# Sums of squares of batches 2 to 4: accumulating DMA transfers in place of VectorE additions

## The chip, the cores and the metric

The kernel runs on one core of one Trainium2 chip, in one launch. The metric is the device time of that launch in microseconds (us), as the median of repeated runs; lower is better.

## What is computed

Channel attention over 4 batches of 6080 tokens with 256 channels, followed by a feed-forward layer with a squared ReLU. Queries and keys are normalised over the tokens, so each batch needs the sum of squares of every channel of q and of k over all 6080 tokens.

```python
qn = q / (norm(q, axis=1) + 1e-06)            # per channel, over the tokens
kn = k / (norm(k, axis=1) + 1e-06)
s = kn.transpose(0, 2, 1) @ qn / tau          # 256 x 256 per batch
a = softmax(s)                                # along the last axis
x = (v @ a).reshape(4 * 6080, 256)
h = maximum(x @ w_in, 0.0)                    # 2048 wide
out = (h * h) @ w_out
```

## The kernel before

The attention matrix of a batch is folded into w_in first (`fold`, `fold7`), so that the large work is two layers of matrix products over v. Each layer uses Strassen's seven products, and every float32 operand is split into a high and a low part of type float32r, so that one product is three matmuls. Tokens are worked in chunks of up to 1024 (6 per batch), and a chunk in 8 steps over the hidden width. Such a step is called a quad; there are 192 (4 batches, 6 chunks, 8 steps), and quad n counts the time of the plan.

A quad issues on TensorE the products of its first layer (L600) interleaved with the second layer of the quad before (L722, or L757 and L799 for the steps that are paired). ScalarE and VectorE empty the banks (L642, L651, L664, L669), square the ReLU (L615, L616, L629) and split the results (L619, L620, L630, L631).

Beside it runs side work for the next batch: `at(u, fn, ...)` gives a step a due time in quads, `run_side` issues the due steps between the products, and `pinned` ties each to ScalarE and VectorE instructions issued some 0.9 quads before. The framework then sets the final order on each engine from priorities, dependencies, buffers that come free and its own estimates of durations; each engine and each DMA queue works its list in order.

The side work for batch b (1 to 3 in the code, counted from 0; the batches 2 to 4 of the title) begins with the scores. Keys and queries come in as tiles `kqt` of four token rows per partition (L202, SyncE's queue). For every pair of rows, `score_split` splits them (L225, L226), `score_burst` issues 12 matmuls (L240), and `score_norm` squares them on ScalarE into a 128x1024 tile `sq` (L219) and adds that on VectorE to the running sum `acc` (L220). The first pair is squared straight into `acc` (L216). That makes 23 additions a batch and 92 in all; batch 0 runs them at the start of the kernel, before the quads.

The tag `sq` has two buffers. They also serve `combine_parts` (L505 to L519), `norms_wide` (L318), `attnT` and `fold7`. When all pairs are in, `squares_split` adds the two halves of `acc` (L303), and norms, exponentials and folds follow. The folded weights are split into tiles `wt` and stored to HBM as `wsc` by GpSimd's queue (POOL; L521); SyncE's queue loads them again one quad at a time (L527). The same POOL queue stores `tsc` (L459) and the outputs (L743).

The pacing of the side work, which sets when a square is due:

```python
first, last = (NJ + 2 if b == 1 else 0), 30
for i in range(NT // 2):                       # NT = 48
    u, k = u0 + first + i * (last - first) // (NT // 2), 2 * i
    ...
    at(u - 0.8, score_norm, b, k)
```

Of the kernel before, what the change touches and what calls it, by code (L numbers as in the profile page):

```python
# [13 lines left out]
ALU = mybir.AluOpType  # L14
# [6 lines left out]
def tile_channel_attention_relu2_ffn(ctx, tc, kq, vT, tau, w_in, w_out, outT):  # L21
# [15 lines left out]
    nc = tc.nc  # L37
# [155 lines left out]
    accs = {}  # L193
# [16 lines left out]
    def score_norm(b, kt):  # L210

        g, t = divmod(kt, G)
        x = kqt[b, g][:, t:t + 2]
        if kt == 0:
            accs[b] = small.tile([P, 2, C2], F32, name="acc")
            nc.scalar.activation(out=accs[b], in_=x, func=AF.Square)  # L216
        else:
            sq = work.tile([P, 2, C2], F32, name="sq", tag="sq")
            nc.scalar.activation(out=sq, in_=x, func=AF.Square)  # L219
            nc.vector.tensor_add(out=accs[b], in0=accs[b], in1=sq)  # L220

    def score_split(b, kt):
        x = kqt[b, kt // G][:, kt % G, :]
# [624 lines left out]
    for kt in range(NT):  # L848
        g = kt // G
        if kt % G == 0 and g < NGK - 1:  # L850
            for t in range(0, G, 2):
                score_norm(0, kt + t)
        if kt == NT - LAST:
            for t in range(0, G, 2):
                score_norm(0, NT - G + t)
            with tc.high_priority():
                summed = sums_of_squares(0)
            decoded = decode_w_in(0)
            with tc.high_priority(), tc.issue_after(decoded):
                scaled = norms(0)  # L860
            with tc.issue_after(scaled):
                fold_split(0, 0)
        with ExitStack() as order:
            if kt >= NT - LAST:
                order.enter_context(tc.issue_after(summed))
            score_mm(0, kt, s0, kt == 0, kt == NT - 1)
        if kt == 3 * G - 1:
            load_tau()
        if kt % G == G - 1:
            load_next()  # L870
# [63 lines left out]
    for b in range(1, B):  # L934
        u0 = (b - 1) * QB
        first, last = (NJ + 2 if b == 1 else 0), 30
        for i in range(NT // 2):
            u, k = u0 + first + i * (last - first) // (NT // 2), 2 * i
            if k % G == 0:
                at(u - 3.4, score_load, b, k // G)  # L940
            at(u - 0.8, score_norm, b, k)
            if b > 1 or k > LATE[-1]:
                at(u - 1.0, score_split, b, k)
                at(u - 0.5, score_split, b, k + 1)
                at(u + MID, score_burst, b, [k, k + 1])
        end = u0 + last
        at(end - 0.6, squares_split, b)
        at(end + MID, norms_wide, b)
        at(end + 1.6, lambda b=b: exps(b, s_acc[b]))
        at(end + 2 + MID, attnT, b)  # L950
        for g in range(0, NG, 2):
            u = end + 3 + 3.5 * g
            if b == 1:
                at(u - 3.5, load_wins2, g)
            for i in range(NP):
                at(u + i - (0.7 if b == 1 else 2.5), right7, b, g, i)
                at(u + i + MID, fold7, b, g, i)
            for i in range(2):
                at(u + NP + 2 * i, combine, b, g + i)
                at(u + NP + 2 * i + 1, combine, b, g + i)  # L960
# [88 lines left out]
```

## Time and profile before

| | us |
|---|---|
| median of 3 runs | 2147.49 |
| lowest and highest of them | 2146.72, 2148.78 |
| the profiled execution's own time | 2145.74 |
| span of its trace | 2143.9 |

| engine | busy us | share of the span |
|---|---|---|
| TensorE matmul (PE) | 2137.1 | 100% |
| TensorE weight load (PEld) | 1764.3 | 82% |
| VectorE (DVE) | 1822.0 | 85% |
| ScalarE (ACT) | 1451.9 | 68% |
| GpSimd (POOL) | 89.9 | 4% |

Times are microseconds from the span's start unless marked ns. "Landing" of a DMA is the time from its issue until its last byte is reported. Matmuls are pipelined and their ends are modelled, so a full TensorE row says that no gap was seen and not that the engine is at its peak. A name such as `acc<-acc,sq` gives the tile written and the tiles read. An idle time is put down to whatever came last before the instruction started.

### The profile page before, as it was taken

What the parts mean: (1) busy time and instruction counts of PE and PEld (TensorE: products, weight loads), DVE (VectorE), ACT (ScalarE), POOL (GpSimd) and SP (SyncE); (2) the same over time, 40 slices, a digit from 0 to 9 for tenths busy, and PEclk for the clock granted to TensorE, in tenths of its full rate; (3) what the DMA queues carried; (4) which work ended last, traced back from release to release, by engine and by line L of the source; (5) the groups of instructions that cost most, each with busy time, mean ns of one, the idle gap of its engine ahead of it and who ended that gap; (6) DMA issues with size and microseconds to landing.
All of it is one profiled execution on the core that took longest, in us unless ns stands there. A gap on an engine that the chain in (4) does not pass through costs nothing.

```text
span 2143.9 us, 27072 instructions
## 1 busy us (share of the span) xinstructions
PE 2137.1 (100%) x9756; PEld 1764.3 (82%) x9756; DVE 1822.0 (85%) x2549; ACT 1451.9 (68%) x2411; POOL 89.9 (4%) x167
## 2 busy tenths in 40 slices
PE   9999999999999999999999999999999999999999
PEld 8878888888888888888888888888888888888888
DVE  7998898989999889897899988989789768768765
ACT  6887677766776767666677676767566656656654
POOL 0110000001000000000000000000000000000000
PEclk9999999999999999999999999999999999999999
DMA  9877755467785554555767546446576655555452
GB/s 370 300 282 259 256 181 189 172 239 262 254 302 208 196 206 160 174 200 212 277 232 287 211 175 218 148 177 219 194 266 235 224 179 189 172 179 182 167 178 84
DMA packets 101557, 461.83 MB, mean 215 GB/s; under 512 B 11824, under 2 KB 14512, under 8 KB 94640
## 3 DMA queue, kind: packets, MB, share of 16 engines
q1 hardware_dynamic: 85152, 391.23, 51.9%
q0 software_dynamic: 16128, 68.76, 8.1%
q8 instruction: 77, 1.26, 0.2%
q14 instruction: 56, 0.46, 0.1%
q10 hardware_dynamic: 144, 0.12, 0.0%
HBM read 390.33 MB, written 69.73 MB: 215 GB/s over the span
## 4 chain that ended last, share of the span: by engine, by line
PE 68%; issue 27%; DMA 1%; POOL 1%; DVE 1%; ACT 1%; POOLq 0%; SPq 0%; DVEq 0%; ACTq 0%
PE o L722 26%; PE h L600 17%; PE z L600 8%; PE x L600 4%; PE x L799 4%; PE o L757 2%; PE h L240 2%; PE x L240 2%; PE o L240 1%; PE o L799 1%; PE h L466 1%; POOL outT L743 1%; DMA wss<-wo 1%; DMA wsc<-wt 0%; DMA wt<-wsc 0%
## 5 line engine op out<-in xcount | busy, mean ns | idle before, releaser
L722 PE MATMUL o<-g,wo 128*128 128x512 f32 (+1 forms) x3552 | 912.2, 388 | 0.2
L722 PEld LDWEIGHTS o<-g,wo 128*128 128x128 f32 x3552 | 664.0, 188 | 136.8 <-DVE g L631 2.9
L600 PE MATMUL h<-vt,wt 128*128 128x512 f32 (+1 forms) x2304 | 620.5, 390 | 0.4 <-DMA wt<-wsc 0.4
L600 PEld LDWEIGHTS h<-vt,wt 128*128 128x128 f32 x2304 | 427.8, 188 | 98.0 <-ACT x L642 12.4
L600 PE MATMUL z<-vt,wt 128*128 128x512 f32 (+1 forms) x1152 | 326.9, 390 | 0.0
L620 DVE TENSOR_TENSOR g<-r,g 128x512 fp32r<-128x512 f32 (+1 forms) x296 | 201.3, 680 | 59.6 <-ACT g L619 58.3
L630 ACT CAST g<-s 128x1024 fp32r<-128x1024 f32 (+1 forms) x148 | 153.7, 1038 | 138.5 <-DVE s L629 138.4
L600 PEld LDWEIGHTS z<-vt,wt 128*128 128x128 f32 x1152 | 210.1, 188 | 43.0 <-DVE pair L669 3.8
L631 DVE TENSOR_TENSOR g<-s,g 128x1024 fp32r<-128x1024 f32 (+1 forms) x148 | 178.9, 1209 | 42.2 <-ACT g L630 41.6
L615 ACT ACTIVATE r<-z 128x512 f32<-128x512 f32 (+1 forms) x148 | 87.5, 591 | 167.1 <-PE z L600 144.0
L616 ACT ACTIVATE r<-r 128x512 f32<-128x512 f32 (+1 forms) x296 | 186.3, 630 | 5.0
L629 DVE SCALAR_TENSOR_TENSOR s<-s 128x1024 f32<-128x1024 f32 (+1 forms) x148 | 178.6, 1206 | 0.9
L600 PE MATMUL x<-vt,wt 128*128 128x512 f32 (+1 forms) x576 | 161.6, 388 | 0.0
L785 ACT CAST th<-pair 128x1024 fp32r<-128x1024 f32 (+1 forms) x88 | 92.0, 1046 | 89.2 <-PE x L799 66.5
L651 ACT COPY z<-h 128x512 f32<-128x512 f32 (+1 forms) x192 | 111.1, 579 | 33.1 <-PE h L600 32.8
L220 DVE TENSOR_TENSOR acc<-acc,sq 128x1024 f32<-128x1024 f32 x92 | 112.4, 1222 | 18.9 <-ACT sq L219 16.7
L600 PEld LDWEIGHTS x<-vt,wt 128*128 128x128 f32 x576 | 108.1, 188 | 22.3
L642 ACT COPY x<-h 128x512 f32<-128x512 f32 (+1 forms) x192 | 111.0, 578 | 5.7 <-PE h L600 5.1
L664 ACT COPY m<-h 128x512 f32<-128x512 f32 (+1 forms) x192 | 110.7, 577 | 1.7 <-PE h L600 0.9
L572 DVE TENSOR_TENSOR vt<-v,vt 128x512 fp32r<-128x512 f32 (+1 forms) x144 | 96.1, 679 | 13.8 <-ACT vt L571 12.7
L631 DVE TENSOR_TENSOR g<-pair,g 128x1024 fp32r<-128x1024 f32 (+1 forms) x44 | 53.5, 1215 | 63.1 <-ACT g L630 63.1
L786 DVE TENSOR_TENSOR th<-pair,th 128x1024 fp32r<-128x1024 f32 (+1 forms) x88 | 106.4, 1209 | 0.6
(201 smaller groups left out, 2729.9 us busy)
## 6 DMA issues: line engine op xcount, KB each, us to landing
wt<-wsc SPq DMA_DIRECT2D x184, 896.0 KB, 4.8
wo<-wosc SPq DMA_DIRECT2D x140, 512.0 KB, 4.3
kqt<-kq SPq DMA_DIRECT2D x47, 1024.0 KB, 7.3
wo<-wss SPq DMA_DIRECT2D x66, 512.0 KB, 5.3
wsc<-wt POOLq DMA_DIRECT2D x32, 896.0 KB, 5.3
v<-vT SPq DMA_DIRECT2D x40, 512.0 KB, 5.9
outT<-res POOLq DMA_DIRECT2D x80, 256.0 KB, 5.2
hl<-tsc SPq DMA_DIRECT2D x28, 512.0 KB, 3.8
```

Of the source, the lines that this page charges most:

```text
L220: nc.vector.tensor_add(out=accs[b], in0=accs[b], in1=sq)
L240: ins = nc.tensor.matmul(out=s[:, h * C:(h + 1) * C], lhsT=l, rhs=r, start=first and h == 0 and n == 0, stop=last and n == len(terms) - 1, ...
L600: nc.tensor.matmul(out=out[:, :T], lhsT=w[:, l, i], rhs=v[:, r, :T], start=start and n == 0, stop=n == 2, skip_group_check=True)
L616: nc.scalar.activation(out=r, in_=r, func=AF.Square)
L620: nc.vector.tensor_sub(out=hl[:, 1, :T], in0=r, in1=hl[:, 0, :T])
L629: nc.vector.scalar_tensor_tensor(out=s, in0=s, scalar=0.0, op0=ALU.max, in1=s, op1=ALU.mult)
L630: nc.scalar.copy(out=h, in_=s)
L631: nc.vector.tensor_sub(out=l, in0=s, in1=h)
L642: ins = nc.scalar.copy(out=st["X"][:, :T], in_=st["B"][:, :T])
L651: ins = nc.scalar.copy(out=st["Z"][:, :T], in_=st["B"][:, :T])
L664: nc.scalar.copy(out=state[q]["m7"][:, :T], in_=H[:, :T])
L722: nc.tensor.matmul(out=ps[:, lo:hi], lhsT=w2[:, l, f, e], rhs=r[:, lo:hi], start=start and k == 0, stop=stop and k == 2, skip_group_check= ...
```

## The change

In batches 1 to 3 (counted from 0) the addition of `sq` to `acc` is taken from VectorE and issued as a DMA from GpSimd's queue that reads the 512 KB tile `sq` and adds it to `acc`, both in SBUF. Batch 0 keeps its additions on VectorE.

```diff
         else:
             sq = work.tile([P, 2, C2], F32, name="sq", tag="sq")
             nc.scalar.activation(out=sq, in_=x, func=AF.Square)
-            nc.vector.tensor_add(out=accs[b], in0=accs[b], in1=sq)
+            if b:
+                nc.gpsimd.dma_start(out=accs[b], in_=sq, accum_op=ALU.add)
+            else:
+                nc.vector.tensor_add(out=accs[b], in0=accs[b], in1=sq)
```

## Rows read from the trace of the kernel before

**Rows 1.** The page's part 1: busy us (share of the span) and instructions of each engine

```profile
PE 2137.1 (100%) x9756; PEld 1764.3 (82%) x9756; DVE 1822.0 (85%) x2549; ACT 1451.9 (68%) x2411; POOL 89.9 (4%) x167
```

**Rows 2.** Stretches of the three batches: PE, PEld, DVE, ACT, POOL busy, clock, DMA share, GB/s

```profile
165.00:387.00 222.00, 221.98 (x1020) 181.93 (x1019) 197.21 (x256) 162.49 (x259) 6.48 (x12) 1.00 0.62 220
570.00:921.00 351.00, 350.91 (x1671) 291.43 (x1672) 315.04 (x431) 246.93 (x408) 10.85 (x20) 1.00 0.58 208
1100.00:1452.00 352.00, 351.52 (x1676) 292.35 (x1675) 315.20 (x432) 247.18 (x408) 10.81 (x20) 1.00 0.57 203
```

**Rows 3.** The chain that ended last, in order of time: start, us, what

```profile
1299.81 2.04 PE o L722 x9
1308.65 1.43 PE h L240 x12
1311.47 2.04 PE o L722 x9
...
1729.49 2.04 PE o L722 x9
1739.69 2.04 PE o L722 x9
```

**Rows 4.** Waits of weight loads, 1100 to 1452: who, for whom, us, times, longest

```profile
PEld o L757 <- DVE g L631: 1.1, 4, 0.3
PEld z L600 <- DVE pair L669: 0.9, 3, 0.3
...
PEld o L722 <- DVE g L631: 0.8, 2, 0.5
```

**Rows 5.** Groups of instructions: the additions (busy us, mean ns, idle time before)

```profile
L220 DVE TENSOR_TENSOR acc<-acc,sq 128x1024 f32<-128x1024 f32 x92 | 112.4, 1222 | 18.9 <-ACT sq L219 16.7
```

**Rows 6.** DMA queues: packets, MB, share of sixteen engines over the span

```profile
q0 software_dynamic: 16128, 68.76, 8.1%
```

**Rows 7.** Line 459, 512 KB stores from POOL: duration ns, first and last start, landing

```profile
L459 POOL DMA_DIRECT2D tsc<-hl x14: 532/534/729, 428.2 to 564.7; - x14
...
DMA to landing us min/median/max: 2.9/4.1/8.0
```

**Rows 8.** Line 155, the eight 512 KB stores wosc<-wo from POOL: landing

```profile
DMA to landing us min/median/max: 4.2/7.2/10.9
```

**Rows 9.** Line 219 in the three stretches: duration ns, first and last start

```profile
L219 ACT ACTIVATE sq<-kqt x23: 1046/1060/1072, 168.9 to 368.1; 128x1024 f32<-128x1024 f32 x23
...
L219 ACT ACTIVATE sq<-kqt x23: 1052/1063/1072, 586.1 to 888.8; 128x1024 f32<-128x1024 f32 x23
...
L219 ACT ACTIVATE sq<-kqt x23: 1052/1064/1080, 1117.6 to 1419.4; 128x1024 f32<-128x1024 f32 x23
```

**Rows 10.** Line 303, the step after a batch's last addition: first and last start

```profile
L303 DVE TENSOR_TENSOR acc<-acc x3: 683/685/685, 385.3 to 1450.0; 128x512 f32<-128x512 f32 x3
```

**Rows 11.** Timeline of ScalarE, fourth batch: start, us, line, operation

```profile
1136.65 1.07 ACT L219 ACTIVATE sq<-kqt 128x1024 f32<-128x1024 f32 x1
...
1140.16 1.07 ACT L219 ACTIVATE sq<-kqt 128x1024 f32<-128x1024 f32 x1
...
1176.15 1.05 ACT L219 ACTIVATE sq<-kqt 128x1024 f32<-128x1024 f32 x1
```

**Rows 12.** Timeline of VectorE, the same stretch: start, us, line, operation

```profile
1138.47 1.22 DVE L220 TENSOR_TENSOR acc<-acc,sq 128x1024 f32<-128x1024 f32 x1
...
1149.27 0.68 DVE L519 TENSOR_TENSOR wt<-sq,wt 128x512 fp32r<-128x512 f32 x1
...
1192.30 1.22 DVE L220 TENSOR_TENSOR acc<-acc,sq 128x1024 f32<-128x1024 f32 x1
```

**Rows 13.** The chain around the first weights of the fourth batch: start, us, what

```profile
1150.25 7.49 DMA wsc<-wt
1157.79 6.49 DMA wt<-wsc
1164.41 1.62 PE h L600 x6
```

## The prediction

> **What bounds the kernel now.** I read the engine shares first. TensorE's matmul row is busy for 2137.1 us of a span of 2143.9, VectorE for 1822.0 and ScalarE for 1451.9 [rows 1]. The additions are VectorE's, and VectorE is not the longest row. A share over the whole span can hide a stage with another limit, so I then took the three stretches in which batches 2 to 4 are squared and added (165 to 387, 570 to 921, 1100 to 1452) [rows 2]. TensorE is busy for 221.98 of 222, 350.91 of 351 and 351.52 of 352 us, at the full granted clock of 1.00; VectorE is at 89% and 90% there, and DMA engines at 0.57 to 0.62. So the stage is TensorE's too.
>
> A full matmul row could hide slow matmuls, since their ends are modelled. The chain in order of time answers that [rows 3]. Late in the kernel, with no additions or scores, the same place in the plan recurs after 1739.69 - 1729.49 = 10.20 us. In the fourth batch's stretch it recurs after 1311.47 - 1299.81 = 11.66 us, with one burst of scores of 1.43 us inside. 10.20 + 1.43 = 11.63, so a quad with additions loses some 0.03 us. About 80 quads lie in the three stretches (925 us / 11.66), which makes some 2.4 us of stalls in all, whoever causes them.
>
> **What goes.** 69 of the 92 additions leave VectorE: 69 x 1.222 = 84.3 us [rows 5]. TensorE covers them. What VectorE costs TensorE is bounded from above by the waits of weight loads on VectorE: in the last stretch 1.1 + 0.9 + 0.8 = 2.8 us [rows 4], and at that rate over all three 2.8 x 925 / 352 = 7.4 us. From below it is nothing, as most weight loads wait behind a running matmul. The pace of the quads is nearer to the matmuls than the weight loads are, and it allows 2.4 us for all causes; I take 1 us of gain. The order on the engines may shift with 69 instructions gone from VectorE's list; the gain and loss from that lie within the same 2.4 us.
>
> **What comes.** POOL issues 69 more transfers, 0.53 us each [rows 7], 37 us on an engine that is busy for 89.9 [rows 1]. Nothing waits for that time itself. SyncE's queue gets no new entry.
>
> The time of one accumulating transfer, L, from issue to landing, is not in this trace. The nearest rows are POOL's plain stores of the same size out of SBUF: 2.9 us at the least, 4.1 in the median, 8.0 at most between 428 and 565 us [rows 7], and 4.2, 7.2 and 10.9 in the first 152 us [rows 8], where the inputs stream in. The new transfer also has to read what it adds to. POOL's queue moved 68.76 MB in 8.1% of 2143.9 us, which is 396 KB per us with all sixteen engines [rows 6], so 512 KB (524,288 bytes) is 1.3 us, and I add that once. The ends for L are 2.9 (the second read free) and 10.9 + 1.3 = 12.2. The traffic of the stretches resembles that of line 459 more than that of the start, so I take 4.1 + 1.3 = 5.4 us. The Trainium skill (DMA: Bandwidth & Descriptors, Anatomy of one DMA) puts a transfer from this queue at about 2.0 us plus bytes at 436 KB per us, which would be an estimated 3.2 us. The median of 4.1 disagrees by a fourth, and by 3.2 us the sum below would come out about 2 us lower.
>
> Each addition must follow the one before, since both change `acc`: POOL waits for the last landing, and stands still with the stores behind it. The plan leaves room: the 23 squares of a batch are (368.1 - 168.9) / 22 = 9.05 us apart in the second batch and 13.8 and 13.7 us in the third and fourth [rows 9]. With 5.4 us the chain keeps up. Stores of outputs and weights behind a waiting addition are late by at most one L.
>
> What is held longer is the buffer `sq`, but not by much: in the kernel before the square of 1176.15 is added only at 1192.30 and holds its buffer for 17 us [rows 11, 12], because VectorE is behind. A transfer frees it after 1.1 + 5.4 us. The exception is a square that follows closely while `combine_parts` holds the other buffer. In the fourth batch the square of 1136.65 was added by 1139.69, and the next could start at 1140.16; the other buffer was read until 1149.95 [rows 11, 12]. With the transfer the buffer comes free at 1136.65 + 1.07 + 5.4 = 1143.1, so ScalarE, if its order stays, stands for 3.0 us. The ends are nothing (L = 2.9 frees it at 1140.6, half a microsecond late) and 9.8 us (L = 12.2). ScalarE empties the banks for TensorE, so part of it reaches the matmuls. There is one such place in the third batch as well. I take 1 us each, 2 us; the ends are 0 and 2 x 9.8.
>
> Of the stores behind POOL's waits one kind is tight. The folded weights were stored at 1150.25, landed 7.49 us later, were loaded again at 1157.79 in 6.49 us, and the matmuls of 1164.41 stood for them [rows 13]. The last addition ahead of that store lands about 1143.1 + 1.1 + 5.4 = 1149.6, so the store is not held back, only the traffic is denser. I take 0.5 us. At the end of a batch VectorE's L303 waits for the last landing; it starts at 385.3 and the last square of that batch ends at 369.2 [rows 9, 10], so 16 us cover the L.
>
> DMA time: 23 transfers of 1.3 to 2.6 us of sixteen engines are 30 to 61 us in the second batch's 222, on a share of 0.62 [rows 2], which becomes 0.76 to 0.89. Loads are issued ahead, so this costs nothing until the share reaches 1.
>
> **Sum.** -1 + 2 + 0.5 = +1.5 us against the profiled execution's 2145.74; its median stands 1.75 us above it (2147.49). That gives 2149.0 us, no change: a measurement of this kernel can tell about 0.2%, 4.3 us, from none. The case's own range is 2144 to 2156.
>
> **Rivals.**
> - *The chain of additions sets the pace (slower).* Place: second batch. If L is over 9.05 us, additions fall behind, both `sq` buffers stay occupied, and ScalarE stands at each square with the copies for TensorE behind it. The price is 23 x (L - 9.05): at 10 us +22, 2170 us; at 12.2 us +72, 2220. For it: the slow rows, 7.2 + 1.3 = 8.5 us in the median [rows 8], and that no row shows the adding itself. Against: the median of rows 7. The Trainium skill (DMA: Bandwidth & Descriptors, Rules for kernel authors) says that an accumulating transfer on the same bytes must wait for the earlier one's completion, so two cannot overlap; no run so far shows it. Chance 0.17.
> - *The DMA engines fill up (slower).* From (1 - 0.62) x 222 / 23 = 3.7 us of all sixteen engines per transfer on, the loads of weights come late in the second batch. At 4.5 us it is 104 + 138 - 222 = +20 us, 2168 us. It needs nearly three times the plain rate's price. Chance 0.08.
> - *VectorE mattered more (faster).* All 7.4 us of waits come back: 2147.49 - 7.4 = 2140.1. The matmul pace speaks against it. Chance 0.05.
> - *The change does less than it says*: additions come to run in another form, or the order is made anew with gains and losses elsewhere; no change then. Chance 0.04.
>
> **Numbers.** The forecast holds 0.66, of which 0.57 within 0.2%, 0.07 slower (ScalarE's stands near their upper end) and 0.02 faster. The chain adds 0.17 to slower, the full DMA engines 0.06 to slower and 0.02 to same, VectorE 0.04 to faster and 0.01 to same, the last 0.04 to same. That makes faster 0.06, same 0.64, slower 0.30. The range runs from 2144 to 2172: it leaves out the gain (0.05), the chain above L = 10 (0.08) and a part of the full engines (0.04).
>
> **What would show it.** VectorE's busy time falls by about 84 us and L220 stays at 23 instructions; POOL has some 69 more issues of `acc<-sq`, landing in about 5.4 us. The matmul row stays full in the three stretches, a quad with a burst stays near 11.6 us, and ScalarE shows waits for `acc<-sq` near 610 and 1140 us of some 3 us each. The forecast is wrong if landings are over 9 us, if ScalarE's waits on them come at most squares, or if the DMA share of 165 to 387 nears 1.

## The result and the profile after

The changed kernel takes 2164.88 us in the median of 6 runs (2157.59 to 2167.8) against 2147.1: a ratio of 1.0078 with an interval of 1.0065 to 1.0091, some 17 us slower. Lines behind the edit have moved down by three, so L600 of before is L603 here, and the transfers are line 221.

The page's part 1 after the change (busy us, share of the span, instructions), to set beside [rows 1]:

```profile
PE 2140.9 (99%) x9756; PEld 1766.1 (82%) x9756; DVE 1751.5 (81%) x2480; ACT 1452.8 (67%) x2411; POOL 150.2 (7%) x236
```

VectorE lost 69 instructions and 70 us (84 were expected; without any additions, further down, it loses 71), POOL gained 69 and 60 us, and TensorE has the same 9756 matmuls in a span of 2161.2 us. The stretches of [rows 2] (PE, PEld, DVE, ACT, POOL busy, clock, DMA share, GB/s) say where the time came from:

```profile
165.00:387.00 222.00, 216.51 (x984) 176.71 (x983) 166.08 (x223) 157.88 (x251) 26.37 (x35) 0.98 0.88 269
570.00:921.00 351.00, 346.84 (x1648) 287.62 (x1647) 287.38 (x406) 243.94 (x400) 31.42 (x44) 1.00 0.74 238
1100.00:1452.00 352.00, 346.73 (x1650) 288.43 (x1649) 287.33 (x405) 243.59 (x399) 31.05 (x43) 1.00 0.75 236
```

TensorE stands for 5.5, 4.2 and 5.3 us there, where it stood for 0.6 us in all before. The DMA share rose from 0.62, 0.58 and 0.57 to 0.88, 0.74 and 0.75. Cut finer, each loss lies in one short piece:

```profile
200.00:250.00 50.00, 44.54 (x184) 35.49 (x183) 38.76 (x52) 33.04 (x51) 5.08 (x6) 0.93 0.87 254
600.00:650.00 50.00, 46.33 (x223) 37.72 (x222) 38.15 (x61) 34.03 (x61) 6.41 (x10) 1.00 0.99 336
1135.00:1185.00 50.00, 44.73 (x215) 36.08 (x214) 35.73 (x57) 31.96 (x59) 6.51 (x10) 1.00 0.93 306
```

These 150 us hold 14.4 us of TensorE's idle time. In the first, the clock column (0.93) adds to it. The waits of the matmuls name the releasers (who, for whom, us in total, times, longest):

```profile
PE x L802 <- ACT r L618: 3.8, 1, 3.8
PE z L603 <- DVE s L672: 3.6, 2, 2.0
PE h L603 <- ACT x L645: 2.5, 1, 2.5
PE x L802 <- DMA wo<-wss: 2.2, 3, 1.7
PE h L603 <- DMA wt<-wsc: 1.5, 2, 1.1
```

There are two kinds: matmuls that wait for ScalarE or VectorE, and matmuls whose weights land late. The timeline shows what stood behind the first kind (start, us, line, operation, idle time before and its releaser). The second batch:

```profile
217.12 1.06 ACT L219 ACTIVATE sq<-kqt 128x1024 f32<-128x1024 f32 x1 [3.87 <-DMA acc<-sq]
...
218.08 0.58 ACT L618 ACTIVATE r<-x 128x512 f32<-128x512 f32 x1
...
218.71 1.22 PE L802 MATMUL x<-th,wo 128*128 128x512 f32 x2 [3.76 <-ACT r L618]
```

The third:

```profile
625.20 1.06 ACT L219 ACTIVATE sq<-kqt 128x1024 f32<-128x1024 f32 x1 [6.30 <-DMA acc<-sq]
...
627.58 0.59 ACT L645 COPY x<-h 128x512 f32<-128x512 f32 x1
...
628.22 0.96 PE L603 MATMUL h<-vt,wt 128*128 128x512 f32 x3 [2.47 <-ACT x L645]
```

And the fourth, where VectorE is the one that stands:

```profile
1142.56 0.42 DVE L510 TENSOR_TENSOR sq<-kqt 128x256 f32<-128x256 f32 x1 [3.90 <-DMA acc<-sq]
...
1145.30 0.68 DVE L672 TENSOR_TENSOR s<-z,m 128x512 f32<-128x512 f32 x1
...
1146.04 0.97 PE L603 MATMUL z<-vt,wt 128*128 128x512 f32 x3 [1.95 <-DVE s L672]
...
1155.83 1.06 ACT L219 ACTIVATE sq<-kqt 128x1024 f32<-128x1024 f32 x1 [1.86 <-DMA acc<-sq]
```

Each time the next user of an `sq` buffer stands at the head of its engine's list until a transfer lands; a bank (a part of the memory that matmuls write to) that TensorE needs emptied is behind it. These are few places: four waits for 69 transfers (the lists of ScalarE's and VectorE's waits: us in total, times, longest):

```profile
ACT sq L219 <- DMA acc<-sq: 12.0, 3, 6.3
DVE sq L510 <- DMA acc<-sq: 3.9, 1, 3.9
```

POOL's own list stands for landings too, since each addition is issued only when the one before it has landed. From 170 to 247 us nine transfers follow one another in this way, each but the first issued 0.5 to 0.9 us after the landing ahead of it. Three of them (start, us, operation, idle time before):

```profile
200.82 0.85 POOL L221 DMA_DIRECT2D acc<-sq  x1 [4.99 <-ACT x L645]
208.86 0.85 POOL L221 DMA_DIRECT2D acc<-sq  x1 [7.19 <-ACT x L645]
217.61 0.85 POOL L221 DMA_DIRECT2D acc<-sq  x1 [7.91 <-issue]
```

The first two landed at 208.34 and 217.09 us. The squares that the second and third of these read were ready at 205.03 and 211.27, so here a buffer is held for the wait as well as for the landing. The nine are 9.6 us apart in the mean, more than the 9.05 us between the squares of this batch before the change [rows 9]. The transfers themselves (line 221: duration ns, first and last start; landing; then the queue's packets, MB and share):

```profile
L221 POOL DMA_DIRECT2D acc<-sq x69: 847/856/942, 170.1 to 1438.4; - x69
...
DMA to landing us min/median/max: 4.5/5.9/12.4
```

```profile
q0 software_dynamic: 26064, 104.94, 16.9%
```

Against [rows 6] the queue takes 0.169 x 2161.2 - 0.081 x 2143.9 = 191.6 us more of the sixteen engines, 2.78 us a transfer.

Two theories stood after this. **Buffer**: `sq` is held until the landing, in the second batch with a wait for its turn before that, and ScalarE or VectorE stand at a few places. **Traffic**: the transfers fill the DMA engines in places (a share of 0.99 from 600 to 650), and the weights of the second layer (`wo<-wss`) and of the first (`wt<-wsc`) land late. A third was that the order which the framework's planner made anew costs time by itself.

### The profile page after: what moved, and what is told of

The parts are those of the page before. It is cut to its first block, busy times and chain, and to the rows that moved or that the text cites. A ratio compares the mean times of both kernels' runs of the same rounds, so it can differ in the third digit from the quotient of the medians.

```text
span 2161.2 us, 27123 instructions
## 1 busy us (share of the span) xinstructions
PE 2140.9 (99%) x9756; PEld 1766.1 (82%) x9756; DVE 1751.5 (81%) x2480; ACT 1452.8 (67%) x2411; POOL 150.2 (7%) x236
## 4 chain that ended last, share of the span: by engine, by line
PE 79%; issue 7%; DMA 4%; POOL 1%; DVE 0%; ACT 0%; POOLq 0%; SPq 0%
PE o L725 31%; PE h L603 20%; PE z L603 10%; PE x L802 5%; PE x L603 5%; PE h L243 3%; PE o L760 3%; DMA acc<-sq 2%; PE o L802 1%; PE h L469 1%; DMA wo<-wss 1%; DMA wsc<-wt 1%; DMA wt<-wsc 1%; POOL outT L746 0%; POOL wsc L524 0%
## 5 line engine op out<-in xcount | busy, mean ns | idle before, releaser
L603 PE MATMUL h<-vt,wt 128*128 128x512 f32 (+1 forms) x2304 | 619.3, 390 | 4.0 <-ACT x L645 2.5
L603 PEld LDWEIGHTS h<-vt,wt 128*128 128x128 f32 x2304 | 428.0, 188 | 101.1 <-ACT x L645 13.7
L603 PE MATMUL z<-vt,wt 128*128 128x512 f32 (+1 forms) x1152 | 327.2, 391 | 4.9 <-DVE s L672 3.6
L603 PEld LDWEIGHTS z<-vt,wt 128*128 128x128 f32 x1152 | 210.1, 188 | 49.3 <-DVE pair L672 5.3
L603 PE MATMUL x<-vt,wt 128*128 128x512 f32 (+1 forms) x576 | 161.4, 388 | 0.0
L603 PEld LDWEIGHTS x<-vt,wt 128*128 128x128 f32 x576 | 108.1, 188 | 22.3
L622 DVE CAST g<-r 128x512 fp32r<-128x512 f32 (+1 forms) x141 | 59.4, 422 | 67.4 <-ACT r L619 67.4
```

Of the source, the lines that this page charges most:

```text
L603: nc.tensor.matmul(out=out[:, :T], lhsT=w[:, l, i], rhs=v[:, r, :T], start=start and n == 0, stop=n == 2, skip_group_check=True)
```

## Experiments

### One batch at a time, and no additions

Transfers in the second batch alone:

```diff
-            if b:
+            if b == 1:
```

> The transfers in the second batch alone; batches 3 and 4 add on VectorE as before. Buffer theory: the stalls near 215 and 245 us stay, with the clock's drop some 7 to 9 us, the ones near 625 and 1145 us go: 2153 to 2157 us. Traffic theory: the second batch has the densest transfers (one per 9 us on a share of 0.62), so it carries most of the loss: 2157 to 2163 us.

Measured: 2157.31 us, ratio 1.0044 (1.0029 to 1.0059). The stalls near 215 and 246 us are there (5.7 us on ScalarE, 2.1 us on `wo<-wss`), and no other of more than 0.6 us. The time lies on the border between the two expectations and decides nothing. In this batch alone the landing, 8.0 us in the median, is far slower than over all three.

Transfers in the third and fourth alone:

```diff
-            if b:
+            if b > 1:
```

> The transfers in batches 3 and 4 alone; the second adds on VectorE. Buffer theory: the stalls where combine_parts shares the sq buffers (near 605 to 650 and 1135 to 1185 us) stay, some 4 and 5 us: 2154 to 2158 us. Traffic theory: a share of 0.57 with one transfer per 14 us has room, so at most 2151 us.

Measured: 2155.04 us, 1.0036 (1.0023 to 1.0049). The two parts add up: 0.44% + 0.36% = 0.80% against 0.78% for the whole. The time is in the buffer theory's range, but the trace shows both kinds; the longest stall of this run is a late load:

```profile
PE h L603 <- DMA wt<-wsc: 6.1, 2, 5.2
PE z L603 <- DVE s L672: 3.7, 2, 1.9
```

It is the load of [rows 13]. Its store was issued at 1159.60 beside loads of tokens and landed after 12.0 us, where it had taken 7.5 before. The trace is of the longest execution of this run (2160.59 us), so this stall may be above its usual size.

No additions at all in batches 2 to 4, so that their sums of squares are those of one pair of rows:

```diff
-            if b:
-                nc.gpsimd.dma_start(out=accs[b], in_=sq, accum_op=ALU.add)
-            else:
+            if b == 0:
                 nc.vector.tensor_add(out=accs[b], in0=accs[b], in1=sq)
```

> The additions of batches 2 to 4 are left out altogether (the sums of squares of those batches are those of one pair of rows); nothing takes their place. It prices what VectorE's 84 us are worth. Buffer and traffic theory alike: 2145 to 2148 us, as TensorE is full. The rival that VectorE mattered more: about 2140 us.

Measured: 2144.83 us, 0.9986 (0.9977 to 0.9995). VectorE's 84 us of additions cost the whole kernel some 3 us (1 to 5 by the interval). That is about the most that moving them can give, as far as one order of the engines shows it.

### Trying to take the hold away

All `sq` and `hl` tiles in one ring of five:

```diff
-    HB = 3
+    HB = 5
...
-            sq = work.tile([P, 2, C2], F32, name="sq", tag="sq")
+            sq = work.tile([P, 2, C2], F32, name="sq", tag="hl", bufs=HB)
```

> The changed kernel with the two sq buffers and the three hl buffers put into one ring of five of the same size; the transfers stay. Buffer theory (ScalarE stands at a few squares, and VectorE once, because the sq buffer is held until the transfer lands, and TensorE stands for them): the waits on acc<-sq go from ScalarE and VectorE, the three stalls near 215, 625 and 1140 to 1160 us go with them, and the time is 2147 to 2152 us. Traffic theory (the DMA engines at a share of 0.9 to 1 make loads of weights late): the same transfers run, so the time stays above 2157 us.

Measured: 2194.0 us, 1.0216 (1.0194 to 1.0238). That is over 2157 us, as the traffic theory had it, but not for the reason that it gave. ScalarE's wait list shows why:

```profile
ACT hl L228 <- DMA acc<-sq: 42.4, 14, 7.7
```

The hold was not taken away but spread: now the splits of tokens, which are due with every burst of scores, draw a buffer that a transfer holds, 14 times. What the shared ring costs without transfers was not run.

The transfers read the token tile, so that tokens and not their squares are added:

```diff
-                nc.gpsimd.dma_start(out=accs[b], in_=sq, accum_op=ALU.add)
+                nc.gpsimd.dma_start(out=accs[b], in_=x, accum_op=ALU.add)
...
-            nc.scalar.copy(out=n2, in_=nps[:, :K + C])
+            nc.scalar.activation(out=n2, in_=nps[:, :K + C], func=AF.Abs)
```

> The same 69 accumulating transfers, but they read the token tile kqt in place of sq, so the square's buffer is free as soon as ScalarE has written it. ScalarE's order is nearly that of the changed kernel. The values added are the tokens themselves and not their squares, and the absolute value is taken ahead of the root. Buffer theory: no engine waits for acc<-sq any more, the stalls near 215, 625 and 1140 to 1160 us go, 2147 to 2152 us. Traffic theory: same bytes, same queue, same times, so 2157 us or more.

Measured: 2184.1 us, 1.0168 (1.0147 to 1.0188). Neither ScalarE nor VectorE waits for a landing, and the time is still well over the changed kernel's. SyncE's queue waits instead, and the matmuls for what stands behind it there:

```profile
SPq L202 <- DMA acc<-kqt: 42.6, 5, 10.4
```

```profile
PE x L802 <- DMA wo<-wss: 20.9, 8, 11.4
```

A load of new tokens needs the tile that the transfer still reads. It waits at the head of SyncE's list, and weight loads that need nothing of it wait behind: in the worst place the token load goes out at 225.61, `wo<-wss` at 226.53, and TensorE resumes at 236.72 after 11.41 us. So this run moved the hold to another list and decides nothing between the theories.

The square written over the tokens, later:

```diff
-            sq = work.tile([P, 2, C2], F32, name="sq", tag="sq")
+            sq = x if b else work.tile([P, 2, C2], F32, name="sq", tag="sq")
...
-            at(u - 0.8, score_norm, b, k)
+            at(u - 0.2, score_norm, b, k)
```

> The square of batches 2 to 4 is written over the token pair in kqt, 0.6 quads later so that the splits have read it, and the transfer adds from there; nothing of the computation changes. Buffer theory: ScalarE no longer stands for a landing, but a token tile is held longer and the square waits for VectorE's split: 2147 to 2155 us. Traffic theory: 2157 us or more.

Measured: 2179.28 us, 1.0147 (1.0133 to 1.0162). The token loads of SyncE's queue wait for landings as in the run before, 29 times and for 199.1 us in all.

A third buffer (`bufs=3` stands at every tile of this tag), with room from the `vt` ring:

```diff
-    VB = 9
+    VB = 8
...
-            sq = work.tile([P, 2, C2], F32, name="sq", tag="sq")
+            sq = work.tile([P, 2, C2], F32, name="sq", tag="sq", bufs=3)
```

> Three sq buffers in place of two; the room comes from the ring of split tokens and v tiles (vt), which has eight in place of nine. Buffer theory: with one more buffer ScalarE's and VectorE's waits on acc<-sq go: 2147 to 2153 us, plus what the smaller ring costs. Traffic theory: 2157 us or more.

Measured: 2158.48 us, 1.0053 (1.0036 to 1.007). ScalarE, VectorE and SyncE wait for no landing here; POOL does, for 23.9 us in three of the transfers. The time is where the traffic theory put it, while the waits went as the buffer theory said. Most of what is left are late loads, at nearly full DMA engines (a share of 0.92, 0.95 and 1.00 in the three pieces of 50 us):

```profile
PE x L802 <- DMA wo<-wss: 3.7, 2, 2.2
PE h L603 <- DMA wt<-wsc: 3.7, 3, 2.3
PE z L603 <- DVE pair L672: 1.8, 1, 1.8
PE h L243 <- DMA vt<-kq: 1.7, 1, 1.7
```

The last row is the smaller ring's own, ahead of all transfers. Its control, the kernel before with eight `vt` buffers:

> Control of the third-buffer run: the kernel before with eight vt buffers in place of nine, all additions on VectorE. If the smaller ring costs something of its own (the stall of 1.9 us near 114 us, a late pair of tokens), 2149 to 2152 us; if the remaining loss of the third-buffer run is all the transfers', 2146 to 2149 us.

Measured: 2151.02 us (2145.59 to 2158.28), 1.0022 (1.001 to 1.0034). The ring costs 0.22%, so the transfers of the third-buffer kernel cost 0.53 - 0.22 = 0.31%, 7 us, where those of the changed kernel cost 0.78%. Buffers account for roughly the difference, 0.47% or 10 us. This is an estimate with some 0.25 points to either side, worked out from the three intervals, and the third buffer also changed the order on the engines, so a part of it may be the order's. The trace of the control is of its shortest execution (2145.59 us); it shows one new stand, of 1.8 us for `vt` near 117 us, and not where the rest of the ring's cost lies.

### Pricing the traffic

The third-buffer kernel with half of each transfer:

```diff
-                nc.gpsimd.dma_start(out=accs[b], in_=sq, accum_op=ALU.add)
+                nc.gpsimd.dma_start(out=accs[b][:, 0], in_=sq[:, 0], accum_op=ALU.add)
```

> The third-buffer kernel with transfers of 256 KB: only the first half of each square is added, the second half of the sums keeps its first pair. Every list of every engine is the same, instruction by instruction, but for the size of the 69 transfers, and no engine waits for them. Traffic theory (what is left of the loss is loads of weights that land late because transfers occupy the DMA engines): the loss against the kernel before falls from 11 us to some 3 to 6, 2150 to 2153 us. Rival (the remaining loss comes from the new order on the engines and queues, or from the smaller ring): 2156 to 2161 us as with whole transfers.

Measured: 2150.8 us, 1.0018 (1.0009 to 1.0027). The order on every engine is that of the third-buffer run, so the 0.53 - 0.18 = 0.35% (7.5 us) between them is the bytes alone; the 0.18% left is no more than the ring's own 0.22%. The stretches of the second and the fourth batch, with whole transfers and then with half of each:

```profile
165.00:387.00 222.00, 218.23 (x994) 178.15 (x993) 167.26 (x226) 158.35 (x251) 26.52 (x35) 0.99 0.89 270
1100.00:1452.00 352.00, 349.74 (x1669) 292.07 (x1668) 290.56 (x409) 246.69 (x406) 31.03 (x43) 1.00 0.75 237
```

```profile
165.00:387.00 222.00, 221.98 (x1019) 181.72 (x1019) 172.52 (x233) 161.90 (x258) 26.61 (x35) 1.00 0.78 245
1100.00:1452.00 352.00, 349.83 (x1666) 292.03 (x1665) 288.96 (x408) 245.28 (x403) 31.03 (x43) 1.00 0.67 218
```

In the second batch the share falls from 0.89 to 0.78 and TensorE is full again; in the third its idle time falls from 4.2 to 0.3 us; in the fourth it is 2.3 and 2.2 us. That is the load of [rows 13] once more: its store takes 11.0 us to land, 10.7 with whole transfers, 7.5 before. So the bytes cost time in the second and third batch, and this late load is not theirs. Halving the bytes also brings the landing from 6.1 to 4.1 us in the median and POOL's waits for it from 23.9 to 3.9 us; how much of the gain comes by that and how much by freer DMA engines was not separated.

For the third-buffer kernel the rival of the new order falls with this, as the order is the same in both; for the changed kernel the next run bounds it.

The changed kernel with plain copies, which leaves out the adding:

```diff
-                nc.gpsimd.dma_start(out=accs[b], in_=sq, accum_op=ALU.add)
+                nc.gpsimd.dma_start(out=accs[b], in_=sq)
```

> The changed kernel with its 69 transfers as plain copies from sq to acc, nothing added (the sums of batches 2 to 4 are those of one pair); all lists of all engines are the same. If the adding itself is dear (2.8 us of all sixteen engines per transfer where a plain one was priced at 1.3): the copies land in about 4 us, cost 1.3 us of engine time, and the time is 2148 to 2155 us. If the price is that of any transfer of this size between two tiles: landing stays near 5.9 us and the time near 2163 us.

Measured: 2152.56 us, 1.0026 (1.0013 to 1.0038). All lists are those of the changed kernel, so two thirds of its loss, 0.78 - 0.26 = 0.52%, come from the adding. The 0.26% left, 5.6 us, holds the new order and the plain copies less VectorE's gain of some 3 us, so the order by itself can cost no more than 8 or 9 us there; it is not shut out. Late loads of folded weights, one in the third batch and one in the fourth, are its longest stalls, and their stores took 11.6 and 11.9 us to land. Those loads, line 221 and the queue:

```profile
PE h L603 <- DMA wt<-wsc: 6.6, 2, 3.4
```

```profile
L221 POOL DMA_DIRECT2D acc<-sq x69: 528/531/542, 169.1 to 1429.8; - x69
...
DMA to landing us min/median/max: 2.8/4.0/11.0
```

```profile
q0 software_dynamic: 26064, 104.94, 12.3%
```

A plain copy takes (0.123 x 2152.5 - 0.081 x 2143.9) / 69 = 1.32 us of the sixteen engines and lands in 4.0 us; an accumulating one takes 2.78 us and 5.9. ScalarE's waits on the landing fall from 12.0 to 3.9 us.

### Transfers only where there is room

Transfers only where squares are far apart and `combine_parts` no longer draws on the `sq` buffers, 38 of the 69:

```diff
-            if b:
+            if b > 1 and kt >= 10:
```

> Transfers only where squares are far apart and combine_parts is done: batches 3 and 4 from their sixth pair on (38 of the 69); the rest adds on VectorE. Buffer theory: no wait for a landing, and the 38 additions taken from VectorE give back up to half of what leaving out all 69 gave: 2144 to 2148 us, at or just under the kernel before. Traffic theory: a share of some 0.73 in those stretches costs nothing or little: 2147 to 2151 us.

> The sparse kernel once more, as its gain was small: 38 transfers in batches 3 and 4 from the sixth pair on. 2143 to 2147 us and a ratio between 0.998 and 1.000 to the kernel before; if the first result was chance, a ratio of 1.000 to 1.002.

Measured: 2145.02 us, 0.9989 (0.998 to 0.9998), and again 2144.99 us, 0.999 (0.9982 to 0.9999). The median is 0.1%, 2 us, below the kernel before, and nearly 20 us below the changed kernel. Neither ScalarE nor VectorE waits for a landing in the first run; POOL does, for 24.0 us in three places. The matmul row is full at a DMA share of 0.73:

```profile
570.00:921.00 351.00, 351.00 (x1675) 292.07 (x1674) 295.67 (x414) 247.27 (x406) 27.46 (x39) 1.00 0.73 236
```

The gain is at the edge of what these runs can tell, as both intervals end just below 1; leaving out all additions gave 0.14%.

## Why the prediction was half right

The measured time lies in the range (2144 to 2172), but not in the likeliest case: "no change" at 0.64 did not come, slower at 0.30 did. It also lies outside the range that the prediction gave for its own case (2144 to 2156). The upper part of the range stands there for two rivals. The condition of the full engines, 3.7 us of all sixteen per transfer, did not come (2.78); that of the chain, more than 9.05 us a transfer, came for the first nine of the 23 transfers of the second batch and not over the whole of it (a landing of 8.0 us in the median). So it is partly luck that the range holds the measured time. The signs of being wrong did not warn either: 11 of the 69 landings took over 9 us but the median did not, ScalarE waited at 3 squares of 69, and the share from 165 to 387 us was 0.88.

- **What bounds the kernel, and what VectorE is worth.** Right. TensorE bounds it, and the gain from VectorE, taken as 1 us with 7.4 as its end, measured some 3 us when the additions were left out.
- **L.** Taken as 5.4 us, 5.9 in the median. The base of 4.1 us was right to 0.1 us (the plain copy: 4.0); the second read was charged 1.3 us and the adding costs 1.9. The estimate of 3.2 us by the Trainium skill (DMA: Bandwidth & Descriptors, Anatomy of one DMA) was low for the copy as well, which took 2.8 us at the least and 4.0 in the median, and the row was the better guide. But a median over all batches hid the spread: 8.0 us in the second batch, and up to 12.4 there.
- **ScalarE's stands.** The mechanism and two of its places were right: a square close behind another while `combine_parts` holds the other buffer, near 610 and 1140 us. The size failed. "I take 1 us each, 2 us" became 10 us or so by the third-buffer comparison. In the third batch ScalarE stood for 6.30 us where 3.0 had been worked out for such a place, and TensorE for 2.47. In the fourth it was first VectorE that stood, since the planner let the square go first and `combine_parts` wait; ScalarE stood for 1.86 us behind that.
- **The chain.** "With 5.4 us the chain keeps up" failed in the first part of the second batch. Nine transfers from 170 to 247 us, with landings of 5.3 to 12.4 us, were 9.6 us apart, and squares start there at 204.0, 210.2 and 217.1 us. When the third of these was due, at some 213.3 us, the transfer of the first was still under way and the second waited for its turn, so both buffers were held and ScalarE stood until 217.1. The rival of the chain had the place and the mechanism, but asked for a mean over the whole batch; a few crowded transfers are enough.
- **DMA time.** "This costs nothing until the share reaches 1" is the step that failed. The share of the second batch was forecast as 0.76 to 0.89 and came out at 0.88 (2.78 us a transfer, where 1.3 to 2.6 were taken), but an average over 222 us says nothing of the short pieces in which transfers and loads coincide, in the third and fourth batch with the stores of folded weights as well. From 600 to 650 us the share was 0.99 in place of 0.75, and loads of `wt` landed after 7.0 us in the median in place of 5.3; from 1135 to 1185 us it was 0.93 in place of 0.72, and they took 8.6 us in place of 6.4. Halving the bytes with every order unchanged gave back 0.35%, 7.5 us; the forecast had 0.5 us for all traffic. A share near 1 does not tell the cost by itself: from 600 to 650 us it is 0.95 with whole and with half transfers in the third-buffer kernel, and TensorE stands for 4.2 us in the one and 0.3 in the other.
- **The first weights of the fourth batch.** Taken as 0.5 us, since "the store is not held back, only the traffic is denser". TensorE stood for that load for 1.06 us in the changed kernel (0.40 before), 2.26 in the third-buffer kernel, 2.17 with half the bytes and 3.40 with plain copies. The store took 10 to 12 us in each of them. As it did so with half the bytes and with plain copies too, the bytes and the adding are not what delays it. Where the early pairs of that batch were added on VectorE it took 7.2 and 7.7 us, and with no additions at all 9.1, so the changed order is a candidate; it was not tested, and the cause stays open.
- **The clock.** No term was set down for it. TensorE stood for 3.76 us up to 218.71, and in the 15 us around it the granted clock was 0.77, between the two levels of 1.2 and 2.4 GHz, where it had been 1.00 before the change (columns as above, after the change and before it):

```profile
215.00:230.00 15.00, 11.29 (x39) 9.13 (x40) 7.48 (x10) 8.17 (x12) 1.69 (x2) 0.77 0.75 207
```

```profile
215.00:230.00 15.00, 15.00 (x67) 12.17 (x67) 14.73 (x19) 9.80 (x14) 0.00 (x0) 1.00 0.60 203
```

A matmul took 11.29 / 39 = 0.289 us there in place of 0.224, so the stall cost some 2.5 us more than its own length. After the 2.47 us of the third batch the clock stayed at 1.00 (625 to 640 us). But the length of one stand does not decide it: in the third-buffer kernel with half transfers, TensorE stood for 2.17 us up to 1171.14, and the clock was 0.66 around it:

```profile
1170.00:1175.00 5.00, 3.86 (x10) 3.06 (x11) 1.28 (x3) 1.84 (x4) 0.00 (x0) 0.66 1.03 321
```

Set against +1.5 us: buffers some 10 us, traffic some 7.5, the clock within these, VectorE -3, which makes 14.5 of the 17 us. The 7.5 us is the price of half the bytes, and the other half and the late load of the fourth batch have no price of their own in this sum; the terms come from runs with intervals of 2 to 4 us and need not add up exactly. The first two are not independent either: late loads hold TensorE for only 3.7 us in the changed kernel's own trace, and a longer landing lengthens the stands of ScalarE and VectorE as well. What stays open is how much of the smaller `vt` ring's cost carries over into the third-buffer run, on which the split between buffers and traffic rests.

## What to carry to other kernels

When work is moved from a compute engine to a DMA, price three things: the time that its source buffer is held (from a few us to over ten, by what else is in flight), which list the next user of that buffer heads (and, where transfers add to one tile, the wait for the one before), and what the DMA engines have to do in the 50 us or so where it collides, and not their share over the stage. An accumulating transfer cost twice the engine time of a copy here. If TensorE is full, such a move can give only what the compute engine's waits cost, some 3 us here; it cost nothing, and gave perhaps 2 us, only at places with room in the buffers and in the DMA engines.

## What the runs showed that was not expected

- An accumulating transfer of 512 KB between two tiles took 2.78 us of the sixteen DMA engines and a plain copy 1.32; POOL needed 0.856 us to issue the one and 0.531 for the other.
- Transfers that add to one tile ran one at a time: nine in a row, each but the first issued 0.5 to 0.9 us after the landing of the one before. ScalarE stood for 3.9 us in that stretch, where it had waited 0.8 us for VectorE's additions.
- Holding a buffer that SyncE's queue has to fill was dearer than holding one of ScalarE's: 32 to 37 us of loss against 17. In the traces weight loads stand behind the token load in one list.
- A stand of TensorE of 3.76 us went with a granted clock of 0.77 over 15 us and one of 2.17 us, in another run, with 0.66 over 5 us; one of 2.47 us went with no drop.
- The store of folded weights of the fourth batch landed after 10 to 12 us in place of 7.5 in each of four kernels with transfers in all three batches, whether they moved all bytes or half, with the add or without.
